# Third buffer for gathered rows, later gate writes and moved requests in an attention and mixture kernel

## The chip, the cores and the metric

The kernel runs on one core of a Trainium2 chip. A core has five engines with queues of their own that meet only at semaphores: TensorE (PE, with its weight loads as PEld), VectorE (DVE), ScalarE (ACT), GpSimd (POOL) and SyncE (SP), which here does nothing but issue DMA transfers. The metric is the device time of one execution in microseconds.

## The reference

```python
# attention on feature maps, 4 x 8 heads of 576 x 64, w_phi 64 x 128
def phi(x):
    proj = x @ w_phi
    proj = proj - max(abs(proj), -1)
    return concatenate([exp(proj), exp(-proj)], -1)
kv = phi(k).T @ v;  z = sum(phi(k), axis=2)
attn = (phi(q) @ kv) / (phi(q) @ z + 1e-06)
x = attn.transpose(0, 2, 1, 3).reshape(2304, 512)
# first mixture: tokens with x @ w_skip > 0, the best of 8 experts
e = argmax(x @ w_gate);  gate = softmax(x @ w_gate)[e]
x = x + gate * relu(x @ w1[e]) @ w2[e]
# second mixture: all 8 experts for every token
P = exp(logits - max);  8 times: P /= P.sum(1); P /= P.sum(0); P *= N / E
out = sum over e of P[:, e] * relu(x @ w1[e]) @ w2[e]
```

## The kernel before

Nearly every float32 operand of a matmul is split into a rounded high part and the remainder (names that end in h and l), and three matmuls take the place of one: high by high, high by low, low by high. So each load is followed by a cast (mostly ACT) and a subtraction (DVE or POOL) before PE can use it.

Four stages follow one another. **Attention** runs in eight units (half `bp` of the tokens, head pair `hp`), software-pipelined; a scheduler orders its steps. Loads are `kt`, `vt` and `qt` (lines 79 to 94); PE transposes them (`pt`), the parts are split (`kh`, `kl`, `qh`, `ql`), and `pp` is the projection with `w_phi` (lines 116 to 118; its operands `wbh` and `wbl` are split from `wb`, a block diagonal of 128 x 256 made at lines 51 to 58). Each unit's output goes to DRAM three times: `xd0` and `xd` (rows to be gathered from) and `x2d` (the tokens that no expert changes).

**Routing** follows each half: DVE makes gates and places, SP writes the gate into one more column of `xd0` and `xd` (line 1229), POOL scatters the token numbers into lists `idx` by nine indirect DMAs (line 487), and DVE makes the table `ti` of each slot's expert and place in the list (line 589).

**The first mixture** (`moe1`) works in slots of 256 tokens of one expert. Slots 0 and 1 run on the first half's tokens while attention ends; the others in `chain(2)`, nested branches whose number is known only when it runs. `fetch(s)` has SP load the slot's list into `ix` (line 614), POOL clear `xg` and gather the 256 rows into it (lines 623, 625) and SP load the first weights (line 634); the second weights follow (line 641). Then PE transposes `xg` (line 660), multiplies by the first weights (`ph`, line 683) and by the second (`py`, line 720). DVE forms `yo` from `py` and `xg`, and POOL scatters `yo` through `ix` into `x2d` (line 728). A slot's last transposes are issued between matmuls of the slot before; `ix` and `xg` have two buffers, chosen by `s % 2`, and both the gather and the scatter read `ix`:

```python
ix, xg = ixs[s % 2], xgs[s % 2]
ins = nc.sync.dma_start(ix, idx[bass.ds(r, SLOT)].rearrange("(a p) o -> p a o", p=P))
```

In slots 0 and 2 this load also waits until all list scatters have landed.

**The second mixture** (`moe2`) is dense. Its first weights are loaded at line 819 into a tile `r`; POOL forms sums and differences of its blocks (lines 831 to 833, 848), ACT splits off `wch` (line 839) and DVE `wcl` (line 846), while PE transposes the token rows `xr`, loaded from `x2d` (line 878), and ACT copies them (`xq`, line 887). Behind them come `pa`, `pb`, `pd` (line 1016) and `py` (line 1052). So that the weights aren't loaded before the slots are done, SP first writes a word `last` into each half of `r` from `xg` (line 817): this marker orders the load behind it. Between the mixtures PE does 90 transposes of a constant (`warm`, line 773).

SP and POOL work through their queues strictly in order: an instruction that waits holds up all behind it.

## Time and profile before

| | us |
|---|---|
| median of 3 runs | 2106.79 |
| lowest and highest run | 2096.18, 2110.84 |
| profiled execution, device time | 2104.46 |
| its span, first to last instruction | 2102.7 |
| PE busy in it | 2017.1 |
| DVE, ACT, POOL busy | 1371.5, 941.0, 522.0 |
| mean granted clock of TensorE, share of full | 0.987 |

The profile is one execution. Its rows name a source line, engine, operation and tiles as out<-in; times count from the first instruction. In a timeline row the first number is the start, the second the time for all that the row holds (x4 is four instructions in a row), and the bracket the idle time of the engine ahead of it with what ended that. SP's rows (SPq) show issues of DMAs, not their transfers. Matmuls are pipelined, so their durations overlap.

### The profile page before, as it was taken

The numbers are of one execution on the slowest core, as the hardware profiler recorded it, in microseconds if no ns is written. First come the engines' busy times: TensorE is split into PE (matmuls) and PEld (weight loads), VectorE is DVE, ScalarE is ACT, GpSimd is POOL, SyncE is SP. The second block draws the span as 40 slices with busy tenths as digits, with TensorE's granted clock in tenths as the row PEclk, the third lists the DMA queues.
The fourth block names the chain that finished last, engine by engine and source line by source line (L and its number), as shares of the span: only waits on it lengthen the run. The fifth ranks groups of instructions, "written<-read, shape, count | busy, mean of one in ns | idle before, by whom it ended". The sixth has DMA issues, their size and how long they took to land.

```text
span 2102.7 us, 29983 instructions
## 1 busy us (share of the span) xinstructions
PE 2017.1 (96%) x11113; PEld 1808.5 (86%) x11113; DVE 1371.5 (65%) x2306; ACT 941.0 (45%) x1893; POOL 522.0 (25%) x382
## 2 busy tenths in 40 slices
PE   6998888999799999999999999999999999999999
PEld 5998777988578999898888998989888888899898
DVE  7888875777557666665665666666575566666663
ACT  4776563554454443343434443443343443343341
POOL 5445334555111112211202111212211111112210
PEclk9999889999999999999999999999999999999999
DMA  4599296564432212213202212212312212212211
GB/s 94 80 126 100 36 209 150 213 217 178 158 106 70 71 50 81 77 45 110 76 31 85 71 51 81 73 48 81 106 46 71 71 51 81 71 50 80 76 56 41
DMA packets 192531, 187.36 MB, mean 89 GB/s; under 512 B 73654, under 2 KB 148150, under 8 KB 192372
## 3 DMA queue, kind: packets, MB, share of 16 engines
q1 hardware_dynamic: 188916, 178.24, 31.7%
q0 software_dynamic: 3456, 7.09, 0.9%
q8 instruction: 90, 1.47, 0.3%
q14 instruction: 69, 0.57, 0.1%
HBM read 163.70 MB, written 23.96 MB: 89 GB/s over the span
## 4 chain that ended last, share of the span: by engine, by line
PE 68%; DMA 11%; DVE 3%; issue 2%; ACT 2%; POOL 1%; SPq 1%; POOLq 0%; DVEq 0%; ACTq 0%
PE py L1052 34%; PE pb L1016 14%; PE pd L1016 9%; PE pa L1016 8%; DMA r<-in_moe_w_dram 5%; DMA x2d<-yo,ix 3%; DMA xg<-xd,ix 1%; PE pg L893 1%; DVE wcl L846 1%; POOL w1l L648 1%; PE ph L683 1%; SPq L819 1%; DMA ix<-idx 0%; ACT w2h L1002 0%; PE py L720 0%
## 5 line engine op out<-in xcount | busy, mean ns | idle before, releaser
L1052 PE MATMUL py<-w2l,hh 128*128 128x512 f32 x1152 | 451.5, 392 | 0.0
L1052 PE MATMUL py<-w2h,hh 128*128 128x512 f32 x1152 | 451.2, 392 | 0.1
L1052 PE MATMUL py<-w2h,hl 128*128 128x512 f32 x1152 | 450.3, 391 | 0.0
L1007 DVE TENSOR_TENSOR w2l<-r,w2h 128x512 fp32r<-128x512 f32 x184 | 169.0, 921 | 216.4 <-ACT w2h L1002 216.4
L1052 PEld LDWEIGHTS py<-w2l,hh 128*128 128x128 f32 x1152 | 216.1, 188 | 48.8 <-issue 0.6
L1052 PEld LDWEIGHTS py<-w2h,hl 128*128 128x128 f32 x1152 | 216.3, 188 | 37.4
L1052 PEld LDWEIGHTS py<-w2h,hh 128*128 128x128 f32 x1152 | 216.3, 188 | 36.3 <-ACT hh L1032 0.4
L1063 DVE SCALAR_TENSOR_TENSOR acc<-py,lg,acc 128x512 f32<-128x512 f32 x264 | 196.9, 746 | 68.7 <-PE py L1052 67.8
L848 POOL TENSOR_TENSOR r<-r,s 128x512 f32<-128x512 f32 x46 | 59.8, 1300 | 650.2 <-DVE wcl L846 638.6
L831 POOL TENSOR_TENSOR s<-r 128x512 f32<-128x512 f32 x46 | 59.2, 1288 | 592.4 <-DMA r<-in_moe_w_dram 592.4
L1002 ACT ACTIVATE w2h<-r 128x512 fp32r<-128x512 f32 x184 | 114.6, 623 | 177.8 <-DMA r<-in_moe_w_dram 177.5
L1032 ACT ACTIVATE hh<-c 128x384 fp32r<-128x384 f32 x192 | 100.9, 525 | 207.5 <-DVE c L1092 115.2
L846 DVE TENSOR_TENSOR wcl<-r,wch 128x512 fp32r<-128x512 f32 x230 | 154.1, 686 | 16.7 <-ACT wch L839 16.4
L1016 PE MATMUL pb<-xch,wch 128*128 128x384 f32 x576 | 149.4, 340 | 8.9 <-ACT v L1024 7.5
L839 ACT ACTIVATE wch<-r 128x512 fp32r<-128x512 f32 x230 | 138.6, 622 | 21.1 <-DMA r<-in_moe_w_dram 11.2
L1016 PE MATMUL pb<-xcl,wch 128*128 128x384 f32 x576 | 147.6, 337 | 0.0
L1016 PE MATMUL pb<-xch,wcl 128*128 128x384 f32 x576 | 147.1, 336 | 0.0
L1076 DVE TENSOR_TENSOR pb<-pb,s 128x384 f32<-128x384 f32 x96 | 54.3, 566 | 122.7 <-PE pb L1016 64.3
L1016 PEld LDWEIGHTS pb<-xch,wch 128*128 128x128 f32 x576 | 104.7, 188 | 30.3 <-ACT v L1024 13.9
L1024 ACT ACTIVATE s<-pa 128x384 f32<-128x384 f32 x96 | 47.2, 491 | 178.0 <-PE pa L1016 178.0
L354 POOL TENSOR_TENSOR fl<-f,fh 128x1024 fp32r<-128x1024 f32 (+1 forms) x40 | 86.5, 2164 | 115.1 <-DVE fh L353 62.1
L846 DVE TENSOR_TENSOR wcl<-s,wch 128x512 fp32r<-128x512 f32 x92 | 63.9, 695 | 73.6 <-ACT wch L839 73.6
(262 smaller groups left out, 4336.5 us busy)
## 6 DMA issues: line engine op xcount, KB each, us to landing
r<-in_moe_w_dram SPq DMA_DIRECT2D x168, 512.0 KB
r<-in_moe_w_dram SPq DMA_DIRECT2D x184, 256.0 KB
xd<-x SPq DMA_DIRECT2D x12, 576.0 KB
qt<-in_q_dram SPq DMA_DIRECT2D x32, 144.0 KB
x2d<-x SPq DMA_DIRECT2D x8, 576.0 KB
xr<-x2d SPq DMA_DIRECT2D x18, 256.0 KB
out_dram<-acc SPq DMA_DIRECT2D x18, 256.0 KB
kt<-in_k_dram SPq DMA_DIRECT2D x32, 128.0 KB
```

Source lines behind the costliest of these rows:

```text
L354: nc.gpsimd.tensor_tensor(fl[:, :n], f[:, :n], f32(fh)[:, :n], ALU.subtract)
L831: g.tensor_tensor(s1, a21, a22, ALU.add)
L839: nc.scalar.activation(h, wsrc[m][i], AF.Copy)
L846: nc.vector.tensor_tensor(l, src[i], f32(h), ALU.subtract)
L848: nc.gpsimd.tensor_tensor(src[3], src[2], src[6], ALU.subtract)
L1002: nc.scalar.activation(h, w2r[m, b], AF.Copy)
L1007: nc.vector.tensor_tensor(l, w2r.pop((m, b)), f32(h), ALU.subtract)
L1016: nc.tensor.matmul(dst, w[:, kb, sl], x[:, kb], start=(start and m == 0), stop=(stop and m == 5), skip_group_check=True,)
L1032: nc.scalar.activation(hh, src, AF.Relu)
L1052: nc.tensor.matmul(py, ht[:, i * P : i * P + P], wt, start=(m == 0), stop=(m == 11))
L1063: nc.vector.scalar_tensor_tensor(accs[t], py, lg[:, t, e : e + 1], accs[t], ALU.mult, ALU.add)
L1076: v.tensor_tensor(b, b, s, ALU.add)
```

## The change

Seven edits are made together.

1. `w_phi` is loaded twice by ACT as it is (`ws`, 64 rows each), with high priority for the scheduler; `wbh` and `wbl` are cleared and each diagonal block is split from `ws`. Before, DVE cleared `wb`, SP loaded both blocks into it, and the whole was split.
2. The four q loads of the first unit are issued by ACT and not by SP.
3. `ix` and `xg` get a third buffer, chosen by `s % 3`. `fill` moves to the pool `rpool`.
4. The gate writes of the first half are issued by `stepped`, a hook that the attention's steps call, at its third call; those of the second half are issued at once, as before.
5. The marker of the second mixture reads the three `ix` tiles and not `xg`: six words in place of two.
6. 80 warm transposes in place of 90.
7. The first weights of the second mixture are split in the order 0, 3, 6, 1, 2, 4, 5 and not 0 to 6; 0, 3 and 6 are the blocks that are used as loaded, and POOL's last difference (line 848) follows the split of block 3.

```diff
-        wb = c1.tile([P, 2 * FH], F32, name="wb")
-        nc.vector.memset(wb, 0.0)
-        nc.sync.dma_start(wb[0:64, 0:FH], w_phi)
-        nc.sync.dma_start(wb[64:128, FH : 2 * FH], w_phi)
+        ws = c1.tile([P, FH], F32, name="ws")
+        with tc.high_priority():
+            for h in range(2):
+                nc.scalar.dma_start(ws[64 * h : 64 * h + 64], w_phi)
...
-        nc.vector.tensor_copy(wbh, wb)
-        nc.vector.tensor_tensor(wbl, wb, f32(wbh), ALU.subtract)
+        with tc.high_priority():
+            for t in (wbh, wbl):
+                nc.vector.memset(f32(t), 0.0)
+        for h in range(2):
+            w, wh, wl = [t[64 * h : 64 * h + 64] for t in (ws, wbh, wbl)]
+            sl = slice(h * FH, h * FH + FH)
+            nc.vector.tensor_copy(wh[:, sl], w)
+            nc.vector.tensor_tensor(wl[:, sl], w, f32(wh)[:, sl], ALU.subtract)
...
-                    nc.sync.dma_start(
+                    (nc.sync if bp or hp else nc.scalar).dma_start(
                         t[64 * b : 64 * b + 64, :, h],
...
-            ix, xg = ixs[s % 2], xgs[s % 2]
+            ix, xg = ixs[s % 3], xgs[s % 3]
...
+        ixs.append(pool.tile([P, 2, 1], I32, name="ix2", bufs=1))
+        xgs.append(pool.tile([P, 2, XW], F32, name="xg2", bufs=1))
...
-        end(xgs[1][0:1, 0, 0:1])
-
-        for _ in range(90):
+        end([t[0:1, 0, 0:1].bitcast(F32) for t in ixs])
+
+        for _ in range(80):
...
-                    nc.sync.dma_start(r[0:1, 0, h, 0:1], last)
+                    for i in range(3):
+                        nc.sync.dma_start(r[0:1, 0, h, i : i + 1], last[i])
...
         for k in range(7):
+            w1_tiles(0, k)
+
+        for k in (0, 3, 6, 1, 2, 4, 5):
             w1_high(0, k)
             w1_low(0, k)
...
+    def stepped():
+        rt.scatter(2)
+        if gates:
+            gates.pop(0)()
...
-        for t in dsts(bp)[:-1]:
-            nc.sync.dma_start(t[:, :, D : D + 1], gate)
+        def go():
+            for t in dsts(bp)[:-1]:
+                nc.sync.dma_start(t[:, :, D : D + 1], gate)
+
+        if bp == 0:
+
+            gates.extend([lambda: None] * 2 + [go])
+        else:
+            go()
```

The lines of the changed file count from 6 (early) to 26 (late) higher. First, SP's queue at the start of the program, before:

```order
L90 DMA kt<-in_k_dram 128x4x64 x2
L62 DMA aug<-in_moe_w_gate_dram 64x8x8
L63 DMA aug<-in_moe_w_skip_dram 64x8x1
L94 DMA kt<-in_k_dram 64x2x64
L90 DMA kt<-in_k_dram 128x4x64 x2
L94 DMA kt<-in_k_dram 64x2x64
L79 DMA qt<-in_q_dram 64x9x64 x2
L1214 DMA idx<-fill 128x160
L79 DMA qt<-in_q_dram 64x9x64 x2
L53 DMA wb<-in_w_phi_dram 64x128
L54 DMA wb<-in_w_phi_dram 64x128
```

and of the change:

```order
L96 DMA kt<-in_k_dram 128x4x64 x2
L100 DMA kt<-in_k_dram 64x2x64
L68 DMA aug<-in_moe_w_gate_dram 64x8x8
L69 DMA aug<-in_moe_w_skip_dram 64x8x1
L96 DMA kt<-in_k_dram 128x4x64 x2
L100 DMA kt<-in_k_dram 64x2x64
L96 DMA vt<-in_v_dram 128x4x64 x2
L100 DMA vt<-in_v_dram 64x2x64
L96 DMA vt<-in_v_dram 128x4x64 x2
L1228 DMA idx<-fill 128x160
L100 DMA vt<-in_v_dram 64x2x64
```

and ACT's queue of the change, which began with the table load before:

```order
L54 DMA ws<-in_w_phi_dram 64x128 x2
L85 DMA qt<-in_q_dram 64x9x64 x4
L76 ACT_TABLE_LOAD
L76 ACTIVATE kh<-pt 128x512 x2
```

SP's four `qt` loads and the two of `wb` are gone from between the second `kt` group and the first `vt`; ACT has six DMAs ahead of its table load.

Second, POOL's queue where slots 0 and 1 end and slot 2 is fetched (`ix_3822` and `ix_3823` are the two buffers before), before:

```order
L648 TENSOR_TENSOR w1l<-r_3826,w1h 128x512 [waits DMAHW6_49,PE_49,Activation_49]
L728 DMA x2d<-yo,ix_3822 2304x512 [waits DMAHW0_49,DMAHW1_49,DMASW6_49,DVE_49]
L728 DMA x2d<-yo,ix_3822 2304x512 [waits DMASW7_49,DMASW6_49,DVE_49]
L623 MEMSET xg_3824 128x1026
L625 DMA xg_3824<-xd,ix_3822 128x513 [waits DMAHW6_49,DMAHW1_49,DMAHW7_49,DMASW0_49,Pool_49]
L625 DMA xg_3824<-xd,ix_3822 128x513 [waits DMASW1_49]
L648 TENSOR_TENSOR w1l<-r_3826,w1h 128x512 [waits DMAHW7_49,PE_49,Activation_49]
```

and of the change (`ix_3821` is slot 0's list, `ix_4196` and `xg_4197` the third buffer):

```order
L654 TENSOR_TENSOR w1l<-r_3825,w1h 128x512 [waits DMAHW6_49,PE_49,Activation_49]
L734 DMA x2d<-yo,ix_3821 2304x512 [waits DMAHW0_49,DMAHW1_49,DMASW6_49,DVE_49]
L631 DMA xg_4197<-xd,ix_4196 128x513 [waits DMAHW6_49,DMAHW1_49,DMAHW7_49,DMASW7_49,Pool_49]
L631 DMA xg_4197<-xd,ix_4196 128x513 [waits DMASW0_49]
L734 DMA x2d<-yo,ix_3821 2304x512 [waits DMASW6_49,DMASW1_49,DVE_49]
L654 TENSOR_TENSOR w1l<-r_3825,w1h 128x512 [waits DMAHW7_49,PE_49,Activation_49]
```

The gathers of slot 2 now stand between the two scatters of slot 0 and not behind both, and the memset has moved out of this stretch, to ahead of three `w2l` of slot 0.

Third, SP's queue behind the branches of the first mixture, with the semaphores that each instruction waits for (DMAHW are transfers issued by SP or ACT, DMASW those issued by POOL), before:

```order
L817 DMA r_9094<-xg_3825 1x1 [waits DMASW4_49,DMAHW7_49,PE_49,Pool_49]
L817 DMA r_9094<-xg_3825 1x1 [waits DMAHW0_49]
L819 DMA r_9094<-in_moe_w_dram 128x4x256 [waits DMAHW7_49,DMAHW1_49]
L819 DMA r_9094<-in_moe_w_dram 128x4x256 [waits DMAHW2_49,DMAHW0_49]
L866 DMA wg<-in_moe_w_gate_dram 128x4x8 [waits DMAHW3_49]
L878 DMA xr<-x2d 128x512 [waits DMASW2_49,DMASW1_49,DMASW3_49,DMASW0_49,DMASW6_49,DVE_49,DMASW7_49,PE_49,DMAHW4_49,Activation_49,Pool_49]
```

and of the change:

```order
L826 DMA r_9095<-ix_3821 1x1 [waits DMAHW6_49,DMAHW5_49,DMAHW7_49,DMAHW4_49,DMAHW3_49]
L826 DMA r_9095<-ix_3822 1x1 [waits DMAHW2_49,DMAHW1_49,DMAHW0_49]
L826 DMA r_9095<-ix_4196 1x1 [waits DMAHW6_49,DMAHW5_49,DMAHW1_49]
L826 DMA r_9095<-ix_3821 1x1 [waits DMAHW2_49]
L826 DMA r_9095<-ix_3822 1x1 [waits DMAHW3_49]
L826 DMA r_9095<-ix_4196 1x1 [waits DMAHW4_49]
L828 DMA r_9095<-in_moe_w_dram 128x4x256 [waits DMAHW5_49,DMAHW7_49,DMAHW1_49,DMAHW0_49]
L828 DMA r_9095<-in_moe_w_dram 128x4x256 [waits DMAHW4_49,DMAHW6_49,DMAHW3_49,DMAHW2_49]
L881 DMA wg<-in_moe_w_gate_dram 128x4x8
L893 DMA xr<-x2d 128x512 [waits DMASW1_49,DMASW2_49,DMASW0_49,DMASW3_49,DVE_49,DMASW6_49,PE_49,DMASW7_49,Activation_49,Pool_49]
```

The marker is six loads instead of two and has lost its waits for POOL, PE and a POOL transfer; the load of `xr` still has them. At the gates, in the middle of attention, SP's two gate writes move from between the x writes and the k loads to behind those k loads, directly ahead of the next unit's four q loads.

## Rows read from the trace of the kernel before

**Rows 1.** Page, part 1, busy time, share of the span and instructions

```profile
PE 2017.1 (96%) x11113; PEld 1808.5 (86%) x11113; DVE 1371.5 (65%) x2306; ACT 941.0 (45%) x1893; POOL 522.0 (25%) x382
```

**Rows 2.** Timeline of SP's issues at the start: start, time for all, line

```profile
8.28 1.21 SPq L79 DMA_DIRECT2D qt<-in_q_dram  x2
10.81 0.49 SPq L53 DMA_DIRECT2D wb<-in_w_phi_dram  x1
```

**Rows 3.** Timeline of PE at the start

```profile
8.20 1.30 PE L105 MATMUL pt<-ident,kt 128*128 128x128 f32 x5 [2.25 <-DMA kt<-in_k_dram]
...
14.27 0.56 PE L116 MATMUL pp<-wbh,kh 128*128 128x256 f32 x1
```

**Rows 4.** Timeline of DVE at the start

```profile
13.61 0.29 DVE L57 CAST wbh<-wb 128x256 fp32r<-128x256 f32 x1 [2.10 <-DMA wb<-in_w_phi_dram]
```

**Rows 5.** Timeline of ACT at the start

```profile
0.81 1.28 ACT L70 ACT_TABLE_LOAD   x1 [0.81 <-PEq L1268]
...
9.32 0.77 ACT L70 ACTIVATE kh<-pt 128x512 fp32r<-128x512 f32 x2 [2.74 <-PE pt L105]
```

**Rows 6.** Stretches: us, busy PE to POOL, PE's clock, DMA share, GB/s

```profile
6.00:8.00 2.00, 0.00 (x0) 0.00 (x0) 0.92 (x3) 0.58 (x1) 0.14 (x1) 1.00 0.73 164
350.00:360.00 10.00, 2.80 (x12) 2.00 (x11) 5.29 (x7) 5.32 (x10) 6.81 (x6) 0.67 0.98 362
550.00:555.00 5.00, 5.00 (x20) 3.99 (x21) 2.48 (x4) 4.54 (x13) 0.00 (x0) 0.51 0.73 240
555.00:600.00 45.00, 43.73 (x216) 28.60 (x215) 26.45 (x43) 26.74 (x52) 5.39 (x4) 1.00 0.48 155
```

**Rows 7.** Timeline of SP at the first gate writes

```profile
188.98 10.63 SPq L1229 DMA_DIRECT2D xd<-gate  x2
```

**Rows 8.** Waits of PE, 180 to 222: us in total, times, longest

```profile
PE pt L105 <- DVE ql L73: 5.8, 1, 5.8
```

**Rows 9.** Waits of SP, 318 to 350

```profile
SPq L614 <- DMA idx<-ids,di: 12.9, 1, 12.9
...
SPq L614 <- DMA x2d<-yo,ix: 4.9, 2, 3.7
```

**Rows 10.** Timeline of SP, slot 2's list

```profile
346.88 0.37 SPq L614 DMA_DIRECT2D ix<-idx  x1
```

**Rows 11.** Timeline of POOL, 320 to 360

```profile
323.80 0.97 POOL L487 DMA_INDIRECT idx<-ids,di  x1 [0.30 <-issue]
...
349.82 1.05 POOL L625 DMA_INDIRECT xg<-xd,ix  x1 [3.88 <-DMA ix<-idx]
```

**Rows 12.** Timeline of PE, slot 2's rows

```profile
357.54 2.30 PE L660 MATMUL pt<-ident,xg 128*128 128x128 f32 x8 [7.07 <-DMA xg<-xd,ix]
...
360.49 0.63 PE L720 MATMUL py<-w2l,hh 128*128 128x512 f32 x1
```

**Rows 13.** Waits of PE, 350 to 552

```profile
PE pt L885 <- ACT xq L887: 6.4, 1, 6.4
...
PE ph L683 <- DVEq L704: 3.3, 1, 3.3
PE py L720 <- DVE w2l L648: 1.8, 1, 1.8
```

**Rows 14.** Timeline of SP at the seam

```profile
532.76 1.43 SPq L817 DMA_DIRECT2D r<-xg  x2
534.53 1.87 SPq L819 DMA_DIRECT2D r<-in_moe_w_dram  x2
```

**Rows 15.** Timeline of PE at the seam

```profile
531.03 11.66 PE L773 MATMUL warm<-ident 128*128 128x128 f32 x90 [4.58 <-PEq L739]
...
549.93 2.98 PE L885 MATMUL pt<-ident,xr 128*128 128x128 f32 x12 [6.36 <-ACT xq L887]
```

**Rows 16.** Timeline of ACT at the seam

```profile
548.18 1.15 ACT L839 ACTIVATE wch<-r 128x512 fp32r<-128x512 f32 x2 [2.04 <-POOL r L848]
```

**Rows 17.** Timeline of POOL at the seam

```profile
540.58 1.27 POOL L831 TENSOR_TENSOR s<-r 128x512 f32<-128x512 f32 x1 [13.07 <-DMA r<-in_moe_w_dram]
```

More of the change, by code (lines that the diff above doesn't have):

```diff
@@ L655, in transposed @@
         def transposed(s, ps0=None):
-            xg, xT = xgs[s % 2], xTs[s % 2]
+            xg, xT = xgs[s % 3], xTs[s % 2]
             for a in range(2):
@@ L712, in product @@
         def product(s, a, hh, hl, between=None):
-            ix, xg = ixs[s % 2], xgs[s % 2]
+            ix, xg = ixs[s % 3], xgs[s % 3]
             py = ps.tile([P, D], F32, name="py", tag="Y")
@@ L834, in sums_w1, with w1_tiles @@
             wsrc[m] = {1: a11, 6: s2, 2: a12, 7: a21, 5: s1, 3: a12, 4: a22}
+        def w1_tiles(m, k):
+            wc[m, ORDER[k]] = [wp.tile([P, 2, QF], F32R, name=nm, tag=nm, bufs=7) for nm in ("wch", "wcl")]
         def w1_high(m, k):
             i = ORDER[k]
-            h, l = [wp.tile([P, 2, QF], F32R, name=nm, tag=nm, bufs=7) for nm in ("wch", "wcl")]
-            nc.scalar.activation(h, wsrc[m][i], AF.Copy)
-            wc[m, i] = (h, l)
+            if (m, i) not in wc:
+                w1_tiles(m, k)
+            nc.scalar.activation(wc[m, i][0], wsrc[m][i], AF.Copy)
         def w1_low(m, k):
@@ L1210, in tile_kernel @@
     xtd = [[dram.tile([D, NTOK // 6], F32, name=f"xt{i}{h}") for h in range(2)] for i in range(2)]
-    with tc.tile_pool(name="fill", bufs=1) as fp:
-        fill = fp.tile([P, NIDX // P], I32, name="fill")
-        nc.gpsimd.iota(fill, [[1, NIDX // P]], base=OOB, channel_multiplier=NIDX // P)
-        nc.sync.dma_start(idx.rearrange("(p a) o -> p (a o)", p=P), fill)
+    fill = rpool.tile([P, NIDX // P], I32, name="fill")
+    nc.gpsimd.iota(fill, [[1, NIDX // P]], base=OOB, channel_multiplier=NIDX // P)
+    nc.sync.dma_start(idx.rearrange("(p a) o -> p (a o)", p=P), fill)
     rt = Router(tc, nc, c, rpool, None, idx)
@@ L1221, in dsts @@
         return [t[rows].rearrange("(p j) d -> p j d", j=NJ) for t in ((xd0, xd, x2d) if bp == 0 else (xd, x2d))]
-    late = []
+    late, gates = [], []
+    def stepped():
+        rt.scatter(2)
+        if gates:
+            gates.pop(0)()
     def route(bp, psum):
@@ L1247, in tile_kernel @@
     attention(
-        tc, nc, c, q, k, v, w_phi, moe_w_gate, moe_w_skip, lgs, routed, lambda: rt.scatter(2),
+        tc, nc, c, q, k, v, w_phi, moe_w_gate, moe_w_skip, lgs, routed, stepped,
         lambda: next(m1), m1.send
```

## The prediction, made before the changed kernel ran

> **What bounds the kernel now.** I read the page's busy times first: PE works 96% of the span [rows 1], so only PE's gaps can be won, and each must be found where it lies. The matmuls themselves are left as they are. Next I read the rows by stretch and the waits of PE, and then the queues behind each wait. The change can reach four gaps: the start, where PE has no weights for its first projections [rows 2 to 5]; the end of the first half of attention, where two gate writes hold SP [rows 7, 8]; slot 2 of the first mixture, where PE waits for gathered rows [rows 9 to 13]; and the seam to the second mixture [rows 13 to 17].
>
> **A, the start.** `wb` is asked for behind the aug, k and q loads: SP issues q at 8.28 and `wb` at 10.81 [rows 2]. The cast of `wb` starts at 13.61 after a wait for that load [rows 4], and the first projection `pp` at 14.27, though its keys' last transposes start at 8.20 and take 1.30 us, to 9.50 [rows 3]. Afterwards ACT asks for `w_phi` as its first instruction, and SP has v behind k (the first order rows). With the weights there, `pp` can start when the keys are split: ACT copies the later pieces from 9.32 on for 0.77 [rows 5], so the matmuls of the first piece can go from 9.5. That is 14.27 − 9.5 = 4.8 us earlier at best. Against it stand two costs. ACT issues six DMAs (two of `w_phi`, four of q) ahead of its table load. The trace has no DMA issued by ACT; the nearest row is SP's, 1.21 us for two [rows 2], so 3.6 us in all, and with 0.8 at the start and 1.28 for the table load [rows 5] ACT comes free at about 5.7, which is early enough; at three times that price it comes free at 12.9 and little is left. And q now travels with the keys. In 6 to 8 us the DMA engines are busy 0.73 of the time [rows 6], so there is some room, and I take 1.3 us off: −3.5; bounds −5 and 0. The next in line, `vh`, isn't late, as the v load moves up by four issues.
>
> A rule of the Trainium skill speaks against this edit (DMA: Bandwidth & Descriptors, Issuing engines are not separate DMA queues): DMAs of several engines run on the same 16 DMA engines and interleave, so only the issuing sequencer's time is saved. By it, q's four loads of 147 KB (64 × 9 × 64 words) would sit between the keys; at 225 GB/s (164 GB/s at 0.73 of the time [rows 6]) they take 2.6 us, A would be −2.2 and the sum 1.3 us smaller.
>
> **B, the gates.** Two writes of one word per token hold SP for 10.63 us from 188.98 [rows 7]; four k loads of the next unit stand behind them. PE then loses 5.8 us in that neighbourhood, but the wait that ends it is for `ql` on DVE, not for k [rows 8]. Two steps on, the k loads go first and the gates stand directly ahead of the next q load. That load has one buffer, which PE must release, so part of the hold is covered. If it isn't, and the same 10.6 us fall on q, I put the loss at up to 3; if the whole wait goes, 5.8 are won. I take −1.5; bounds −6 and +3.
>
> **C, the third buffer.** PE waits 7.07 us at 357.54 for the rows of slot 2 [rows 12]. Back through the queues: the gather is issued at 349.82 [rows 11], because the list's load is issued at 346.88 [rows 10], because SP had waited 12.9 us for the lists to be complete and then 4.9 us for the two `x2d` scatters of slot 0, whose buffer the list goes into [rows 9]. The third buffer takes the 4.9 away and not the 12.9: the last list scatter is issued at 323.80 [rows 11] and, by 346.88 − 4.9, lands near 341.9, 18 us later, in a stretch full of weight loads. So the list's load moves up by 5 us, and the gather with it, which now stands ahead of the second `x2d` scatter on POOL (the second order rows). PE's idle time becomes 7.1 − 5 = 2.1 us. The gap also costs clock: the granted clock is 0.67 in 350 to 360 [rows 6], so half speed in its later part, and after it 8 transposes take 2.30 us, and `py` 0.63 each [rows 12], where the mean of full-speed transposes is 0.13 (1.0 for 8, from the warm ones' 11.66 / 90 [rows 15]). For the transposes and the 12 `py` behind them I put the loss at about 3 us. With 2 us of idle time I expect most of it back: C1 = −5 − 2.5 = −7.5; bounds −3 (the lists land later still) and −10.4 (the whole gap and its clock). Weights of slot 2 are asked for 5 us earlier by the same move, so they aren't late next.
>
> In later slots SP waits for `x2d` in the same way, but PE hardly does: in 350 to 552 it loses 3.3 us ahead of `ph` and 1.8 ahead of `py` [rows 13], for splits of weights that are asked for behind the list. Weights asked for earlier should end most of it. C2 = −3; bounds 0 and −5.1. The price is one more memset on POOL, which has a wait for PE alone and stands where POOL is free.
>
> **D, the seam.** SP's marker reads `xg`, so it waits for the last gather and for POOL; it is issued at 532.76 and the first weights of the second mixture at 534.53 [rows 14]. PE starts 90 warm transposes at 531.03, which take 11.66 us, and 8 of `xr`, and then waits 6.4 us before the transposes at 549.93 [rows 13, 15]: ACT is at `wch` until 548.18 + 1.15 [rows 16] and only then copies `xq`. Afterwards the six markers read lists that have long been loaded, so SP issues them when it leaves the branches. Its last weight loads of a slot that isn't run must have landed by then; I put that near 521. Six markers at 1.43 / 2 [rows 14] are 4.3 us, so the weights are asked for at about 526, and ACT has the raw blocks before POOL leaves the branches. POOL's three sums start after its exit, which the marker's 532.76 shows, at 1.27 each [rows 17], to 536.6; its last difference follows directly, because the raw blocks are split first. That puts the last `wch` near 539.5, ahead of the end of the warm transposes, 531.03 + 80 × 0.13 = 541.4. The 20 transposes of `xr` with ACT's copies between take some 3.5 more, so that they end at 545, against 549.93 + 2.98 = 552.9 [rows 15]: −8 at best. Against it: `xr` is still asked for only when `x2d` is complete, near 533 (the third order rows). I take −7; bounds −2 (`xr` or POOL's sums are what ACT waits for) and −11. In 555 to 600 PE is busy 43.7 of 45 us [rows 6], so what is won stays won.
>
> **Sum.** −3.5 − 1.5 − 7.5 − 3 − 7 = −22.5 against the profiled execution, 2104.46 us: 2082. The median of the runs, 2106.79, is 2.3 us above that, in a spread of 14.7; I make no correction. About 1%, 21 us, is what a measurement of this kernel can tell from no change, so the forecast, 0.988 of the median, lies just on the far side.
>
> **Rivals.**
> 1. *Half of it is hidden or not reached* (2093). q between the keys and ACT's issues leave the start −1.5, B gives 0, C its 5 us and neither clock nor later slots, and the seam is bound by `xr` (−5): −11.5. For it: the lists' late scatter and `xr`'s wait for `x2d` both survive the change. Against: the first wait of the seam is the marker's alone.
> 2. *The lists were slow by accident* (2075). The last list scatter needs 18 us to land. If it lands early after the change, C1 is −10.4, and with A at −5 and D at −9 the sum is −29. For it: 4-byte scatters among weight loads; against: the weight loads keep their places.
> 3. *The clock drops in the seam* (2087). With ten transposes fewer PE may stand idle behind the warm ones as it does now, 6.4 us [rows 13], after which the granted clock is 0.51 [rows 6] and 12 transposes take 2.98 us [rows 15]. If `xq` is as far behind the warm ones as now, D is only the ten transposes, −1.3, and the sum −17. The Trainium skill has the same consequence of an idle stretch (TensorE: Matmul & The Clock Gate, Part 1: The HAM clock gate): half clock until the engine has been kept busy again.
> 4. *Slower* (2110). The list scatter that survives decides alone. If the earlier loads crowd it so that it lands at 369 and not at 341.9, slot 2 waits 27 us more and keeps its half clock (2.5), and the sum is +7. It decides from 21 us on, at 363; no scatter of the trace comes near that.
>
> **Chances.** Forecast 0.48, rival 1 0.25, rival 2 0.12, rival 3 0.12, rival 4 0.03. The likeliest is 2082; its terms' bounds, taken as independent, give about ±8. The range reaches over rivals 1 to 3 with some of the runs' spread: 2069 to 2099. Faster by over 1% means under 2085.7: rival 2, two thirds of the forecast, some of rivals 3 and 1 through the spread: 0.53. Slower by over 1%: 0.02. Within 1%: 0.45.
>
> **What would show it.** A: first `pp` at 9.5 to 11, ACT's first `kh` at about 6. B: gate writes behind the k loads, and PE's wait for `ql` under 5.8. C: the list's load of slot 2 released by the list scatter and not by `x2d`; PE idle about 2 us ahead of slot 2's transposes, at full clock. D: `r<-in_moe_w` issued some 6 us ahead of POOL's exit, and `pa` directly behind the transposes. The forecast is wrong if ACT's DMAs take far more than 0.6 us, if the lists land late again, or if PE still waits for `xq`.

## The result, and the profile after

The changed kernel took 2086.04 us (median of 6 runs, 2079.86 to 2089.64) against 2104.23 for the kernel before (6 runs beside them): ratio 0.9911, 95% interval 0.9883 to 0.9939. It is 0.9% faster, with an interval clear of 1, though within the 1% that the prediction counts as no change, and 4 us above the forecast of 2082. The profiled execution took 2085.24 us and its span fell from 2102.7 to 2083.5, by 19.2 us where the sum said 22.5. The matmuls cost what they did, by the page's busy times (compare [rows 1]):

```profile
PE 2017.4 (97%) x11103; PEld 1810.0 (87%) x11103; DVE 1359.2 (65%) x2309; ACT 940.8 (45%) x1893; POOL 520.3 (25%) x382
```

To see where the time came from, I compared the start of the same matmuls in both traces. "Lead" is after minus before, so negative is earlier; times are those of the profile before.

| stage, up to | lead at its end | this stage | forecast |
|---|---|---|---|
| start and first units, 180 | +0.7 | +0.7 | A: −3.5 |
| around the gates, 275 | −2.9 | −3.6 | B: −1.5 |
| end of attention, first slots, 346 | −4.9 | −2.0 | none |
| slot 2, 430 | −10.4 | −5.5 | C1: −7.5 |
| later slots, 509 | −6.9 | +3.5 | C2: −3 |
| seam, 552 | −15.8 | −8.9 | D: −7 |
| second mixture, end | −19.5 | −3.7 | none |

So the total is near the forecast, but A and C2 have the wrong sign, C1 is smaller than forecast, B and D are larger, and 5.7 us were not forecast at all.

**The start.** ACT's timeline (start, time for all, line; ACTq is its issuing of DMAs) answers [rows 5], PE's [rows 3]:

```profile
0.81 1.20 ACTq L54 DMA_DIRECT2D ws<-in_w_phi_dram  x2
2.04 6.54 ACTq L85 DMA_DIRECT2D qt<-in_q_dram  x4
...
9.91 0.60 ACT L76 ACTIVATE kh<-pt 128x512 fp32r<-128x512 f32 x1
```

```profile
11.25 0.78 PE L122 MATMUL pp<-wbh,kh 128*128 128x256 f32 x2
```

The two loads of `w_phi` cost ACT 0.6 each, as assumed, but the four of q 1.64 each, where SP needed about 0.6 [rows 2]. ACT is held for 8.6 us and its first `kh` comes at 9.91, not 6. `pp` starts at 11.25, which is 3.0 earlier than at 14.27. At 42 us the lead is still −2.9, and then it is lost in one place. POOL, PE and a stretch (us, busy PE to POOL, PE's clock, DMA share, GB/s) there:

```profile
47.23 2.66 POOL L162 TENSOR_TENSOR vl<-vt,vh 128x1152 fp32r<-128x1152 f32 x1 [2.61 <-ACT vh L161]
49.85 2.33 POOL L360 TENSOR_TENSOR fl<-f,fh 128x1024 fp32r<-128x1024 f32 x1
```

```profile
52.24 0.33 PE L187 MATMUL kv<-fl,vh 64*65 64x256 f32 x1 [3.48 <-POOL fl L360]
```

```profile
55.00:60.00 5.00, 5.00 (x23) 4.19 (x23) 2.91 (x5) 2.84 (x6) 0.57 (x1) 0.53 0.23 31
```

In the unit's order that the scheduler now makes, POOL does the remainder of v (`vl`) ahead of the remainder of the features (`fl`); before, `fl` started at 50.79 and `vl` at 53.11. PE wants `fl` first, waits 3.48 us (1.55 before), and then runs at a granted clock of 0.53, half of full speed. By 58 us the lead is +2.3.

The prediction credits the gain of `pp` to the moved requests, but it doesn't need them. In the trace of before, the loads of `wb` wait for DVE to clear `wb`, and DVE waits for a transfer out of `fill`:

```profile
10.51 0.27 DVE L52 MEMSET wb<- 128x256 f32 x1 [3.20 <-DMA idx<-fill]
```

SP issues the loads of `wb` directly behind this, at 10.81 [rows 2]. With `fill` in `rpool` (edit 3) that wait is gone with the old requests too, as the first experiment shows.

**The gates.** SP's timeline and PE's waits from 180 to 222 (us in total, times, longest), against [rows 7, 8]:

```profile
190.16 4.53 SPq L100 DMA_DIRECT2D kt<-in_k_dram  x1
194.73 3.88 SPq L96 DMA_DIRECT2D kt<-in_k_dram  x2
198.65 1.84 SPq L100 DMA_DIRECT2D kt<-in_k_dram  x1
200.59 2.06 SPq L1249 DMA_DIRECT2D xd<-gate  x2
```

```profile
PE pt L111 <- DVE ql L79: 3.2, 1, 3.2
```

The two writes hold SP for 2.06 us, not 10.63, and PE's wait is 2.6 us shorter. But the hold has moved rather than gone: the four k loads that now stand where the gate writes stood take 10.25 us from 190.16 on, and behind the gate writes they had taken 3.5:

```profile
199.66 1.59 SPq L94 DMA_DIRECT2D kt<-in_k_dram  x1
201.29 1.28 SPq L90 DMA_DIRECT2D kt<-in_k_dram  x2
202.61 0.63 SPq L94 DMA_DIRECT2D kt<-in_k_dram  x1
```

So the k loads are all issued 2.7 us earlier, at 200.49 and not 203.24, and the next q loads at 212.90, where it was 212.58.

**Slot 2.** Waits of SP from 310 to 345, the issues of the list's load and of the gather, and PE at the gathered rows, against [rows 9 to 12]:

```profile
SPq L620 <- DMA idx<-ids,di: 17.2, 2, 8.9
```

```profile
337.10 0.37 SPq L620 DMA_DIRECT2D ix<-idx  x1
```

```profile
340.08 1.04 POOL L631 DMA_INDIRECT xg<-xd,ix  x1 [11.59 <-DMA ix<-idx]
```

```profile
347.93 0.63 PE L666 MATMUL pt<-ident,xg 128*128 128x128 f32 x4 [2.42 <-DMA xg<-xd,ix]
```

SP's wait for `x2d` is gone and the one for the lists has remained, now the only one ahead of the load. PE waits 2.42 us, and 0.49 more for the second half of the rows, and not 7.07. Its transposes run at full speed: 0.63 for four, where eight took 2.30. The products behind them don't:

```profile
350.53 0.63 PE L726 MATMUL py<-w2h,hh 128*128 128x512 f32 x1
```

The granted clock is 0.50 from 350 to 353, and this `py` takes what it took before the change [rows 12]; from 353.4 on one takes 0.40.

**Later slots.** PE's waits from 330 to 545, and the longest of them in the timelines of DVE, POOL and PE:

```profile
PE py L726 <- DVE w2l L654: 4.3, 2, 3.0
...
PE pt L666 <- DMA xg<-xd,ix: 2.9, 2, 2.4
PE ph L689 <- DVEq L710: 2.4, 1, 2.4
```

```profile
460.76 8.22 DVE L654 TENSOR_TENSOR w2l<-r,w2h 128x512 fp32r<-128x512 f32 x1
```

```profile
460.93 3.81 POOL L654 TENSOR_TENSOR w2l<-r,w2h 128x512 fp32r<-128x512 f32 x3
464.70 3.73 POOL L654 TENSOR_TENSOR w1l<-r,w1h 128x512 fp32r<-128x512 f32 x3
```

```profile
469.03 0.61 PE L726 MATMUL py<-w2l,hh 128*128 128x512 f32 x1 [3.03 <-DVE w2l L654]
```

The wait for `w2l` has grown from 1.8 [rows 13] to 4.3. It isn't that weights come late: DVE has started the subtraction, which takes 0.69 elsewhere, and it lasts 8.22, until six subtractions of POOL, one close behind the other, are over: POOL's end at 468.43, DVE's at 468.98. A shorter one, 6.30 us at 435.62, stands beside POOL's burst of the slot before.

**The seam.** SP, PE and ACT, against [rows 14 to 16]:

```profile
506.49 3.90 SPq L826 DMA_DIRECT2D r<-ix  x6
510.55 1.30 SPq L828 DMA_DIRECT2D r<-in_moe_w_dram  x2
```

```profile
523.63 10.62 PE L781 MATMUL warm<-ident 128*128 128x128 f32 x80 [4.14 <-PEq L745]
534.09 1.04 PE L900 MATMUL pt<-ident,xr 128*128 128x128 f32 x8
...
537.57 0.62 PE L1031 MATMUL pa<-xch,wch 128*128 128x384 f32 x2
```

```profile
532.35 0.63 ACT L852 ACTIVATE wch<-r 128x512 fp32r<-128x512 f32 x1 [1.13 <-POOL r L860]
```

The weights are asked for 13 us ahead of the warm transposes; before it was 3.5 us behind their start. ACT is done with `wch` at 532.98, a microsecond ahead of the first transposes of `xr`, and of the wait of 6.4 us for `xq` 0.5 is left.

### The profile page after: what moved, and what is told of

Same layout as the page of the kernel before. It is cut to its first block, busy times and chain, and to the rows that moved or that the text cites. A ratio compares the mean times of both kernels' runs of the same rounds, so it can differ in the third digit from the quotient of the medians.

```text
span 2083.5 us, 29972 instructions
## 1 busy us (share of the span) xinstructions
PE 2017.4 (97%) x11103; PEld 1810.0 (87%) x11103; DVE 1359.2 (65%) x2309; ACT 940.8 (45%) x1893; POOL 520.3 (25%) x382
## 4 chain that ended last, share of the span: by engine, by line
PE 69%; DMA 2%; DVE 2%; ACT 1%; SPq 0%; issue 0%; DVEq 0%; ACTq 0%
PE py L1067 36%; PE pb L1031 14%; PE pd L1031 9%; PE pa L1031 9%; DMA r<-in_moe_w_dram 2%; PE pg L908 1%; PE warm L781 1%; SPq L828 0%; ACT w2h L1017 0%; DVE wcl L858 0%; PE pt L900 0%; DVE w2l L1022 0%; ACT xch L964 0%; DMA xr<-x2d 0%; DVE hl L1052 0%
## 5 line engine op out<-in xcount | busy, mean ns | idle before, releaser
L1052 DVE SCALAR_TENSOR_TENSOR hl<-c,hh 128x384 fp32r<-128x384 f32 x192 | 106.7, 556 | 7.2 <-ACT hh L1047 7.2
```

What stands on the lines that cost most here:

```text
L1052: nc.vector.scalar_tensor_tensor(hl, src, 0.0, f32(hh), ALU.max, ALU.subtract)
```

## The experiments

Each run changes one thing of the changed kernel unless the text says otherwise. Ratios are to the kernel before on the same chip, with the 95% interval. "Lead" is now against the changed kernel's trace.

**The start undone.** Edit: loads and split of `w_phi` as before, q by SP.

```diff
-                nc.scalar.dma_start(ws[64 * h : 64 * h + 64], w_phi)
+        nc.sync.dma_start(wb[0:64, 0:FH], w_phi)
+        nc.sync.dma_start(wb[64:128, FH : 2 * FH], w_phi)
...
-                    (nc.sync if bp or hp else nc.scalar).dma_start(
+                    nc.sync.dma_start(
```

> The change with its start undone: w_phi and the first q loads by SP, as before. In the two traces PE is 3.0 us ahead of before at 45 us and 0.7 to 1.0 us behind it from 65 us on, because PE waits 3.5 us for POOL's fl (1.55 before) and then runs at half clock. Theory (the gain of the start is given back by POOL doing vl ahead of fl in the second unit, an order that comes with the moved requests): first pp near 14.3, no long wait for fl near 50 us, and from 65 to 180 us PE 0 to 1 us ahead of the changed kernel; whole time the same within 2 us. Rival (the start's gain is real and the loss at 50 us has nothing to do with it): PE 3 us behind the changed kernel from 65 us on, whole time 3 us longer.

Measured: 2085.66 us, 0.9915 (0.9889 to 0.9941). DVE's clearing of `wb` and the first `pp`:

```profile
0.94 0.27 DVE L52 MEMSET wb<- 128x256 f32 x1 [0.94 <-PEq L1288]
```

```profile
10.21 0.78 PE L116 MATMUL pp<-wbh,kh 128*128 128x256 f32 x2
```

The expected 14.3 for `pp` is missed: with the old start it comes at 10.21, 1.0 earlier than in the changed kernel and 4.1 earlier than before. `wb` is cleared at 0.94 and SP asks for it at 1.60. Of the edits that are left, the move of `fill` is the only one that touches what the clearing had waited for; no run makes this move alone. PE is 1.7 later than the changed kernel at 46 us, but 2.0 to 2.4 earlier from 60 to 180: `fl` (49.61) stands ahead of `vl` (52.00) again. So edits 1 and 2 together lose 2 us, and without them `pp` comes forward all the same.

**Only q back to SP.**

```diff
-                    (nc.sync if bp or hp else nc.scalar).dma_start(
+                    nc.sync.dma_start(
```

> The change with only the q loads given back to SP; w_phi stays with ACT. ACT issued its four q loads in 6.54 us, 1.6 each, and its first kh came at 9.91 against 5.99 before. Theory (ACT's issues cost what w_phi won): ACT's kh near 6, first pp near 9.5 to 10 and not 11.25, POOL's fl ahead of vl in the second unit, and PE 3 to 5 us ahead of the changed kernel from 65 to 180 us; whole time about 4 us shorter. Rival (the keys or the DMA engines set the first pp, or the loss at 50 us has another cause): PE within 1 us of the changed kernel from 65 us on.

Measured: 2085.26 us, 0.9896 (0.9852 to 0.994). ACT, PE and POOL:

```profile
6.20 0.60 ACT L76 ACTIVATE kh<-pt 128x512 fp32r<-128x512 f32 x1 [2.88 <-PE pt L111]
```

```profile
9.05 0.78 PE L122 MATMUL pp<-wbh,kh 128*128 128x256 f32 x2
```

```profile
48.26 2.36 POOL L360 TENSOR_TENSOR fl<-f,fh 128x1024 fp32r<-128x1024 f32 x1 [3.25 <-PE pt L111]
50.82 2.43 POOL L162 TENSOR_TENSOR vl<-vt,vh 128x1152 fp32r<-128x1152 f32 x1 [0.21 <-ACT vh L161]
```

`kh` comes at 6.20 and `pp` at 9.05, 2.2 earlier than with q by ACT, 1.2 earlier than with the old start and 5.2 earlier than before; `fl` is first again. This is the start as the prediction had it. The 2.2 themselves don't last: at 42 us the lead is +0.5. It falls to −3.7 between 50 and 66, where POOL now does `fl` first, and is −3.1 to −3.8 up to 165. So q on ACT spoilt the start through the order of the second unit that came with it; no run changes that order alone. At the end of the program little is left in this execution (−0.3): a third hold-up of `w2l` in the slots took 1.6, and what lies behind 510 us took 1.8.

**The gates at once**, as before.

```diff
-        if bp == 0:
-            gates.extend([lambda: None] * 2 + [go])
-        else:
-            go()
+        go()
```

> The change with the first half's gates written at once, as before. Between 195 and 220 us PE went from 0.7 us behind before to 2.9 ahead. Theory (the gate writes' hold of SP did it): SP is held some 10 us at the gates again, PE's wait for ql near 5.8 us again, and PE 3 to 4 us later from 220 us on; whole time 3 to 4 us longer. Rival (the scheduler's order around it did it): PE within 1 us of the changed kernel from 220 us on.

Measured: 2088.79 us, 0.9922 (0.9897 to 0.9948). SP is held for 9.46 us again, and PE goes from −0.5 to +1.4 at 240 us and +3.0 at 270. That has B's sign, but this stretch moves by as much where the gates are alike: among the kernels here with late gates its length differs by −3.8 to +4.7 us, while the gate writes take 2.0 to 2.3 in all. PE's wait for `ql` is 4.4 us here, and 2.7 to 5.6 in the ones with late gates. So B is 2 to 4 us in these two pairs of traces, and not shown clear of that spread.

**Two buffers.**

```diff
-            ix, xg = ixs[s % 3], xgs[s % 3]
+            ix, xg = ixs[s % 2], xgs[s % 2]
...
-                    for i in range(3):
+                    for i in range(2):
```

> The change with two buffers, all else kept (the marker reads two lists). Theory (the third buffer gains 5.5 us in slot 2 and gives back 3.5 later, because the early weight loads delay the x2d scatter that holds POOL, and with it the w2 splits): PE's wait for gathered rows near 7 us, PE 5 to 6 us later than the changed kernel at 365 us, but only 1 to 3 us later at 520; no wait for w2l of 3 us; whole time 1 to 3 us longer. Rival (the waits for w2l in the later slots have another cause): they stay, and the whole time is 5 to 6 us longer.

Measured: 2092.58 us, 0.9931 (0.9908 to 0.9954). PE's waits from 330 to 505:

```profile
PE pt L666 <- DMA xg<-xd,ix: 6.1, 1, 6.1
PE py L726 <- DVE w2l L654: 4.2, 3, 3.1
```

The wait for gathered rows is back, and PE goes from −0.9 ahead of it to +3.1 at 350, 4.0 later. The wait for `w2l` stays at 4.2, so the theory is wrong in this: the third buffer doesn't make it.

**All of `w2l` on VectorE.** From slot 2 on POOL no longer takes three of the eight parts of a slot's `w2l`, so the burst of six gets shorter.

```diff
-                split_w(w2h[:, f], w2l[:, f], r2[:, f], f, s != 1)
+                split_w(w2h[:, f], w2l[:, f], r2[:, f], f, s == 0)
```

> The change with the remainders of the second weights formed by DVE alone from slot 2 on (POOL took three of eight). In the changed kernel one such subtraction of DVE takes 8.22 us at 460.8, as long as six of POOL's stand back to back beside it, against 0.69 alone; PE then waits 3.0 us for it. Theory (DVE can't run its two-input instruction while POOL's run one after another; the bunching on POOL comes from its wait for the x2d scatter): no w2l over 3 us, PE's waits for w2l in 350 to 500 under 1 us (4.3 now), whole time 3 to 5 us shorter. Rival (the second weights land late): the waits stay, DVE's instructions are short and idle time stands ahead of them.

Measured: 2076.24 us, 0.9894 (0.9857 to 0.9932). The groups of `w2l` on DVE from 330 to 510 (count | busy us, mean ns | idle before), first of the changed kernel, then of this run:

```profile
L654 DVE TENSOR_TENSOR w2l<-r,w2h 128x512 fp32r<-128x512 f32 x40 | 47.3, 1183 | 3.5
```

```profile
L654 DVE TENSOR_TENSOR w2l<-r,w2h 128x512 fp32r<-128x512 f32 x64 | 44.4, 694 | 6.1
```

and all of PE's waits from 330 to 505 in this run:

```profile
PE ph L689 <- DVEq L710: 1.9, 1, 1.9
PE ph L689 <- ACT xTh L668: 0.7, 1, 0.7
```

DVE does 24 subtractions more in 2.9 us less, and PE waits for `w2l` nowhere. At 510 us PE is 10.6 earlier. Of that 3.3 was there at 355 already, because in this execution the gathered rows were in time; 7.3 come between 430 and 505. That is more than the 4.3 of the two waits: in the changed kernel the granted clock also fell, to 0.57 from 469 to 473, behind the longer one.

**The same edit in the kernel before.**

> The kernel before with the remainders of the second weights formed by DVE alone from slot 2 on. In the trace of before one such subtraction takes 7.0 us, at 446.1, beside five of POOL's, and PE waits 1.8 us for w2l. Theory (the hold-up is there before the change too, but mostly once, and is not made by the third buffer): no w2l over 2 us, PE's wait for w2l gone, whole time 1 to 4 us shorter than before. Rival (only the change's earlier loads bunch POOL's work): the same time as before within 1 us.

Measured: 2099.1 us, 0.9982 (0.9966 to 0.9999). The kernel before had one such hold-up (7.00 us at 446.09) and loses it: its `w2l` wait is gone, PE is 3.8 earlier at 510. So the hold-up was there before the change, and the changed kernel has more of it. I counted `w2l` of 6 us and more: 1 before, 2 to 3 in the changed kernel and in each of the six variants that leave POOL its share, none in the six runs without.

**Two buffers, `w2l` on VectorE.** Both edits above.

> The change with two buffers and with the remainders of the second weights formed by DVE alone from slot 2 on: what the third buffer is worth when POOL can't hold DVE up in the later slots. Against e8_w2l_by_dve. Theory (the third buffer is worth slot 2's wait and nothing later): PE 4 to 8 us behind e8_w2l_by_dve at 370, the same distance within 2 us at 510; whole time 4 to 8 us longer. Rival (it also speeds the later slots once DVE is free): the distance grows by over 2 us between 370 and 510.

Measured: 2084.78 us, 0.9906 (0.9877 to 0.9936). Against the run with three buffers and `w2l` on VectorE, PE goes from +3.6 ahead of slot 2 to +11.8 at 351, and stays within 0.2 of that until 513. Its wait for the rows, from 330 to 505:

```profile
PE pt L666 <- DMA xg<-xd,ix: 5.3, 1, 5.3
```

So with the hold-ups out of the way two buffers cost 8.2 us, wait and clock, in slot 2 of this pair, and nothing in the later slots. The 8.2 isn't the third buffer's price alone, for in this run with three the rows came in time: the kernel with the old start and `w2l` on VectorE, below, also has three buffers, comes to slot 2 with a lead of 5.3 over that run, waits 5.2 us there and leaves it 2.8 behind. Over all kernels here PE waits 5.3 to 7.1 us for the rows with two buffers (four kernels) and 0 to 5.2, on average 2.9, with three (ten).

**The marker from `xg`.**

```diff
-        end([t[0:1, 0, 0:1].bitcast(F32) for t in ixs])
+        end([xgs[1][0:1, 0, 0:1]])
...
-                    for i in range(3):
+                    for i in range(1):
```

> The change with the old marker: the second mixture's first load is tied to gathered rows (xg) again, one word per half. Between 520 and 560 us the changed kernel won 8.9 us. Theory (the marker is most of it: the weights were asked for at 510.6, 15 us ahead of POOL's exit): weights asked for at about 527, PE idle some 5 to 6 us behind the 80 warm transposes, PE 6 to 7 us later than the changed kernel at 560. Rival (the split order and the fewer warm transposes won it): under 3 us later.

Measured: 2096.51 us, 0.9971 (0.9944 to 0.9999). SP at the seam, and PE's wait from 500 to 570:

```profile
527.43 1.41 SPq L826 DMA_DIRECT2D r<-xg  x2
529.20 1.90 SPq L828 DMA_DIRECT2D r<-in_moe_w_dram  x2
```

```profile
PE pt L900 <- ACT xq L902: 4.1, 1, 4.1
```

The weights are asked for 18.7 us later, the wait for `xq` returns, and PE goes from +2.0 at 510 to +10.5 at 560: the marker is worth 8.5 us, the largest single piece of the change. It is the only piece that the whole times show too: this interval lies just above that of the changed kernel (0.9883 to 0.9939).

**Weights split in the order 0 to 6.**

```diff
-            w1_tiles(0, k)
-
-        for k in (0, 3, 6, 1, 2, 4, 5):
```

> The change with the first weights of the second mixture split in the old order. Theory (the warm transposes cover it: the last wcl ends at 534.7, the first transposes of the token rows start at 534.1): PE within 1.5 us of the changed kernel at 560. Rival (the order is part of what the seam won): 3 us later or more, with PE waiting for xq behind the warm transposes.

Measured: 2086.64 us, 0.9936 (0.9915 to 0.9957). The last two `wch` start at 535.50, behind the first `xq` and no longer ahead of them, and PE waits 0.92 where it waited 0.20:

```profile
537.25 1.20 PE L897 MATMUL pt<-ident,xr 128*128 128x128 f32 x8 [0.92 <-ACT xq L899]
```

PE goes from −0.2 at 510 to +1.9 at 560, so the order is worth 2.1, between the theory's bound and the rival's. It is hardly clear of chance: in kernels whose seam has this order and the marker from `ix` the same stretch differs by up to 1.7 from the changed kernel's.

**Two of them together: q by SP and `w2l` on VectorE.**

> The last edit and the q loads given back to SP, together. If both losses were what the single runs show, PE is 3 to 4 us ahead of the changed kernel at 180 us and 7 to 9 us ahead at 520; whole time 6 to 9 us shorter than the changed kernel, 0.987 to 0.989 of before. Rival (what one wins the other stage gives back): no more than 4 us.

Measured: 2075.81 us, 0.9895 (0.9857 to 0.9932). PE is 4.5 to 5.3 earlier from 58 to 166, 13.4 at 510 and about 10 from 1800 on.

**The old start and `w2l` on VectorE.**

> The change without its first two edits (w_phi and first q loads by SP, as before) and with the remainders of the second weights formed by DVE alone from slot 2 on. Theory (the moved requests are worth nothing or cost 2 us, the split on DVE wins 6 to 10): the whole time 2 us shorter than e8_w2l_by_dve, or the same. Rival (the requests by ACT are worth something once the later slots run freely): 2 us longer or more.

Measured: 2080.65 us, 0.9891 (0.9863 to 0.9919). Against the run with the new start and `w2l` on VectorE, PE is 1.6 to 2 earlier from 66 to 166 here as well, and 3.4 to 6 later from 530 to the end, after a wait of 5.2 for the rows of slot 2. The whole times of the three runs aren't to be told apart.

**60 warm transposes, with q by SP and `w2l` on VectorE.**

```diff
-        for _ in range(80):
+        for _ in range(60):
```

> The changed kernel with q requested by SP, all casts of w2 by VectorE, and 60 instead of 80 warm transposes in the seam. In the run with q by SP and w2 by VectorE the 80 took 10.58 us from 510.71, the last transposes ran from 521.12, pa came at 524.61, and ScalarE was done with the weights' part at 519.5. Theory (the warm ones are now the last to end before pt, so a quarter of them is on the path): they end some 2.6 us sooner, PE then waits up to 1 us for xr's columns, pa comes 1 to 2 us earlier relative to the attention side, at a granted clock near 1.00; time 2074 to 2076, not to be told from 2075.8 by the times alone. Rival (the warm ones keep the clock up; fewer let it fall): granted clock near 0.5 behind them, the transposes and pa run at twice their time, and pa comes as late as before or up to 4 us later. Rival (ScalarE's cast ends last either way): pa does not move.

Measured: 2078.25 us, 0.9885 (0.9861 to 0.9909). PE with 80 and with 60:

```profile
510.71 10.58 PE L781 MATMUL warm<-ident 128*128 128x128 f32 x80 [4.60 <-PEq L745]
521.12 1.04 PE L900 MATMUL pt<-ident,xr 128*128 128x128 f32 x8
...
524.61 0.61 PE L1031 MATMUL pa<-xch,wch 128*128 128x384 f32 x2
```

```profile
513.95 8.44 PE L781 MATMUL warm<-ident 128*128 128x128 f32 x60 [4.44 <-PEq L745]
522.23 1.04 PE L900 MATMUL pt<-ident,xr 128*128 128x128 f32 x8
...
525.71 0.62 PE L1031 MATMUL pa<-xch,wch 128*128 128x384 f32 x2
```

From the first warm transpose to `pa` it is 13.90 with 80 and 11.76 with 60: 2.1 us, a little more than expected, at full speed behind them (1.04 for eight transposes in both). The rival of a falling clock is wrong at this size. ACT ends `wch` at 522.6 and the transposes begin at 522.23, so by these rows fewer still would win little. The whole time doesn't show it: in the second mixture this execution waits 10.6 us, in ten places, for ACT's `v`, and the one with 80 waits 6.3, in four.

## Why the prediction was right or wrong

**A failed** (−3.5 forecast, +0.7 found), in three of its steps. The first is the cause of the late weights: "`wb` is asked for behind the aug, k and q loads". I read SP's order as the reason, and didn't look at what SP's load itself waited for, DVE's clearing of `wb` at 10.51, which waited 3.20 us for the transfer out of `fill`. With the old requests and `fill` moved, `pp` comes at 10.21. So the gain that I credited to ACT's requests comes without them, by an edit that has no term in the sum.

The second is a price. The step "the nearest row is SP's, 1.21 us for two" put ACT's six issues at 3.6 us; they took 7.74, because q's four cost 1.64 each there. The text's other bound, three times the price, is nearly what the four loads cost (2.7 times). With q by SP `pp` is at 9.05, 0.45 earlier than the 9.5 that I gave as the best.

The third turned the term to a loss and was not considered at all: the scheduler's order in the second unit, `vl` ahead of `fl` on POOL. The order of the changed kernel could have been read there. At 165 us the lead over the kernel before is −1.3 and −1.5 in the two kernels with the old start, −1.8 to −3.9 in the three with `w_phi` by ACT and q by SP, and +0.1 to +0.7 in the seven with both by ACT; only these last have `vl` first.

By the rule that I set against this edit (the Trainium skill, DMA: Bandwidth & Descriptors, Issuing engines are not separate DMA queues) A would have been −2.2, through q's transfers among the keys. The trace agrees in part: PE's first transposes of the keys start at 5.77 with q by ACT and at 5.08 with q by SP, 0.7 later. The larger part of the cost is another, ACT's own time: its first `kh` comes 3.7 later (9.91 and 6.20).

**B came out with the forecast's sign, but not by its mechanism.** The gate writes' own hold fell from 10.63 to 2.06 and PE's wait by 2.6. But SP was then held at the k loads, 10.25 us for four, which neither of the two cases of that paragraph (the hold falls on q, the hold goes) allows for. Nor does PE's wait for `ql` follow the gates: with late gates it is 2.7 to 5.6 us, with early ones 3.1 to 5.8. The −3.6 in the two traces and the 2 to 4 in the run with early gates lie within what the stretch varies by anyway, so B's size stays open.

**C1 held by its steps; its clock term was too large** (−7.5 forecast, −5.5 found). The wait for `x2d` went and the wait for the lists stayed. PE's idle time fell by 4.2 to 2.9 us, 2.4 of it in one piece, where 2.1 was forecast. The clock gave 1.3 and not 2.5: the transposes got their full speed back, but the first `py` behind them run at half of it as before. With the third buffer alone taken away slot 2 cost 4.0 us more, and 8.2 in a pair in which the rows of the other run came in time. The wait for the rows is what varies. Since the lists' landing ends SP's wait, this is rival 2's mechanism; it came nearly in full in three runs (waits of 0 and 0.9 us), not in the changed kernel's profile. Rival 4, lists that land later still, came in none.

**C2 failed** (−3 forecast, +3.5 found). The failing step is the reading of two waits, 1.8 for `w2l` and 3.3 for DVE's queue, as "splits of weights that are asked for behind the list". I took the named releaser for lateness of its input and didn't look at how long the releaser itself ran: the kernel before has a `w2l` of 7.00 us at 446.09, ten times the usual, beside POOL's burst. Earlier weights can't shorten that. The wait for DVE's queue was 2.4 in the changed kernel, and is 1.9 in every kernel with `w2l` on VectorE, with two buffers as with three. The six runs without POOL's share of `w2l` have none of it, and with it gone the third buffer neither wins nor loses in the later slots.

The Trainium skill (SBUF — State Buffer, Who interferes with whom) states a rule that fits: VectorE instructions with two inputs in SBUF and GpSimd instructions that read SBUF need one shared read interface, and the one that comes second is blocked until the first has finished. The runs agree that the two engines collide, and go further: DVE's 8.22 us span six of POOL's instructions of about 1.25 us, not one. Why the changed kernel meets the burst oftener than the kernel before (2 or 3 times against once) isn't settled; moved loads shift ACT's and POOL's casts against each other, and no run isolates that.

**D was right and undersized** (−7 forecast, −8.9 found). The steps held: the marker's release, the weights ahead of the warm transposes, `pa` directly behind the transposes of `xr`. I had put the weights at 526; they are asked for at 510.55, since SP issues the markers from 506.49 on, earlier than the 521 that I assumed. `xr` didn't become the bound. Rival 3 is wrong, there being no idle stretch behind the warm transposes. Undone alone, the marker is worth 8.5 and the order 2.1; both with ten transposes at 0.11 are more than the 8.9 together. One piece undone can also spoil what the others win; that this is the reason isn't shown.

**The sum** was right to 3 us because errors cancelled: A and C2 were 10.7 too good, and B, D, the end of attention and the second mixture gave 9.7 more than forecast; C1 2.0 less. Rival 1, half of it hidden, was nearer for the start and for the slots together (−5 against −10.5, found −2.0), and wrong about the gates, where it gave 0, and the seam, where it gave 5. The drift of −3.7 in the second mixture, whose code is unchanged, is not explained; among the runs of the variants the same stretch differs from the changed kernel's by −2.3 to +7.1.

**Better than both**: `w2l` on VectorE, with or without q by SP, at 2076 us, by the medians 10 us below the changed kernel. By the ratios to the kernel before it is less, 0.9894 against 0.9911, under 4 us, and the intervals (0.9857 to 0.9932, and 0.9883 to 0.9939) overlap. So the gain over the changed kernel rests on the traces, where the hold-ups and PE's waits for them are gone, and on a neighbour: beside it on the same chip ran the changed kernel with its weights split in the old order, and the slowest of the four runs with `w2l` on VectorE (2080.15) is faster than the fastest of its ten (2082.89). The kernel with 60 warm transposes has the lowest ratio, 0.9885 (0.9861 to 0.9909), not to be told from these.

## What to carry to other kernels

When a wait names a releaser, look at that instruction's own duration before concluding that its input is late: one of ten times its usual time was held by another engine here, and moving loads didn't help it. When a load comes late, look first at what its issue waited for; here that was a clearing behind a transfer of another tile. Price a DMA's issue by a row of the same engine and shape, and where there is none, keep it off an engine whose first result starts the program. A hold of a queue can move to the next instructions when the one that it stood at is moved away. A third buffer paid at the one place where the queues waited for the second, here one slot of all; what orders a load (the marker) was worth more than the buffer in the whole time.

## What the runs showed of the hardware that was not expected

- The issue of one q load (64 × 9 × 64) took ACT 1.64 us and SP 0.61 to 0.64 in the same stretch of the program; the two of `w_phi` took ACT 0.60 each. It isn't a constant of SP either: a k load that took it 0.63 us in most places took 4.53 at 190.16.
- A subtraction of VectorE with both inputs in SBUF (0.69 us) took 8.22 us beside six back-to-back subtractions of GpSimd, and 6.30 and 7.00 beside five. In the run with `w2l` on VectorE, GpSimd does three in a row with VectorE's `w1l` beside them, and four of these take 5.44 us, 1.36 each: slowed to twice, but served in between.
- The list scatters, of four bytes a token, decide when slot 2 starts: the load that waits for all of them was issued 13.3 us behind the last scatter's start in the changed kernel (323.79 to 337.10), and in the kernel before they had landed some 18 us after it. That isn't the change's doing: in the kernel before with `w2l` on VectorE it is about 13.9, and in the other kernels with three buffers 11.8 to 15.3.
